# A fused attention and feed-forward kernel: V earlier in the prologue, transposes in separate PSUM tiles, V of one batch loaded in blocks, and a last tile in halves

## The chip, the cores and the metric

The kernel runs on one core of one Trainium2 chip. The metric is device microseconds of one execution. Each kernel is run several times on one chip beside the kernel before, and each run also leaves the span of the core and the mean clock that TensorE was granted. The span in a profile is 1.7 to 1.9 us shorter than the time of the same run. Positions "at 72 us" are counted from the start of the span.

## The reference

Eight batches of eight heads, 576 positions, head size 64: causal attention in a sliding window of 64. Its result, read as 4608 rows of 512, goes through a feed-forward stage (FFN) in which two products are multiplied by each other.

```python
scores = scale * np.matmul(q, k.transpose(0, 1, 3, 2))
mask = (rel >= 0) & (rel < 64)                      # rel = query - key position
attn = softmax(np.where(mask, scores, -1e9))
x = np.matmul(attn, v) -> (4608, 512)
a = x @ w1                                          # 512 x 1024
b = x @ w2
h = a * b @ w3                                      # 1024 x 1024
out = h @ w_out                                     # 1024 x 512
```

There is nothing non-linear behind `a * b`, so the kernel folds `w3 @ w_out` into one matrix of 1024 x 512 first, and each group of 512 rows then needs `a`, `b` and one product with the folded matrix.

## The kernel before

The order on each engine is the order in which the program writes it. Loads that cast to fp16 go through GpSimd's queue; K and Q of later batches come over SyncE's queue as fp32 and are cast on an engine. K, Q and V are transposed on TensorE into a PSUM tile and copied to SBUF by VectorE or ScalarE. V loaded as rows (`load_rows`) is transposed twice, to bring positions onto partitions; V loaded in blocks (`load_v`) comes from DRAM in its final place. The masks run on GpSimd.

```python
def load_v(b, *blocks):                              # V in blocks: no cast, no transpose
    vh = v_heads(b)
    for c in blocks:
        lo = D if c == 4 else 0
        s0 = VBLK[c] + lo
        nc.gpsimd.dma_start(out=vh[lo:P, c], in_=v[b, :, s0:s0 + P - lo, :].rearrange("h s d -> s h d"))

def transposes(b, which, *cs, into=None, cps=None):  # 6 transposes and one copy for each third c
    ...
    if into is None:
        into = [ps_t.tile([P, 6, P], FP16, name="tp")]      # ps_t has one buffer
    for c, tp in zip(cs, into):
        for i in range(6):
            nc.tensor.transpose(tp[:, i, :], t16[:, 6 * c + i, :], ident16)
    ...
    for c, tp, cp in zip(cs, into, cps):
        cp(dst..., tp...)

def scores(d):                                       # 16 matmuls, exp on ScalarE, masks on GpSimd
    ...
    nc.scalar.activation(pt[:, :, :, 0:w], s_ps[:, :, :, 0:w], AF.Exp, bias=-SHIFT, scale=scale)
    ...
        nc.gpsimd.affine_select(...)                 # two for each tile (four for a first tile)

def ffn_o(g, t):
    ab = abs_[g]
    o_ps = ps_f.tile([P, DM], FP32, name="f_ps")
    for fc in range(8):
        nc.tensor.matmul(o_ps, ab[:, fc, t * P:t * P + P], wc_sb[:, fc, :], start=(fc == 0), stop=(fc == 7))
    o_sb = sb.tile([P, DM], FP32, name="t2k", bufs=3)
    dve_cp(o_sb, o_ps)
    r0 = g * GT + t * P
    stores.append((r0, o_sb))

def spare(pool, name):                               # two places of one tile
    t = pool.tile([P, 2, 1024], FP16, name=name)
    return [t[:, i, 0:768].rearrange("p (i n) -> p i n", i=6) for i in range(2)]

def keep_busy(n):                                    # filler: computes nothing
    d = ps_t.tile([P, P], FP32, name="tp")
    for _ in range(n):
        nc.tensor.matmul(d, ident16, ident16, start=True, stop=True)
```

The prologue (batch 0 and the folding of the weights), cut:

```python
keep_busy(75)
tps = spare(ps_s, "s_ps") + spare(ps_v, "o_ps")
...                                                  # K of batch 0: cast, transpose, copy
keep_busy(10)
...                                                  # Q of batch 0 likewise
keep_busy(15)
scores(0)
keep_busy(12)
scores(1)
keep_busy(12)
fold_t(0)                                            # transposes of a piece of w3
scores(2)
fold_t(1, act_cp)
fold_mm(0, 0, dve_cp)                                # 8 matmuls of the folding
scores(3) ... scores(5)                              # with fold_t(2), fold_t(3), fold_mm(1..3, 0)
load_rows(1, "v")
keep_busy(12)
cast_qk(0, "v", 0, dve_cp)
cast_qk(0, "v", 1, dve_cp)
transposes(0, "v", 0, 1, 2, into=spare(ps_v, "o_ps") + [tp_bank()], cps=[dve_cp, act_cp, dve_cp])
...                                                  # rest of the folding, values(0..5)
transposes(1, "k", 0, 1, 2, into=spare(ps_s, "s_ps") + [tp_bank()])
ffn_ab(0, 0)                                         # first FFN matmuls
```

The stage after it, in which the first FFN group runs beside the attention of batch 1 and the preparation of batch 2:

```python
steps = [ffn_ab(0, 6), ffn_ab(0, 7)] + [ffn_o(0, t) for t in range(4)]     # shortened
for d in range(6, 12):
    values(d, ps_s if d in (9, 11) else None)
    if d < 9:
        scores(d + 3)
    steps.pop(0)()
    store()
    if d == 6:
        load_v(2, 4, 5)
        load_qk(3, "k")
    if d < 10:
        cast_qk(2, "kq"[(d - 6) // 2], d % 2, pool_cp)      # K of batch 2 is cast on GpSimd
    if d == 9:
        transposes(2, "k", 0)
    if d == 10:
        transposes(2, "k", 1)
transposes(2, "k", 2)
...
transposes(2, "q", 0, 1, 2, into=spare(ps_v, "o_ps") + spare(ps_s, "s_ps")[0:1])
```

Of the kernel before, what the change touches and what calls it, by code (L numbers as in the profile page):

```python
# [8 lines left out]
FP32 = mybir.dt.float32  # L9
FP16 = mybir.dt.float16  # L10
# [134 lines left out]
def kernel(  # L145
# [106 lines left out]
    def transposes(b, which, *cs, into=None, cps=None):  # L252

        t16 = t16s[which, b]
        if cs[0] == 0:
            turned[which, b] = sb.tile([P, NJ, S], FP16, name=which + "T", bufs=1 if which == "v" else 2)
        dst = turned[which, b]
        if into is None:
            into = [ps_t.tile([P, 6, P], FP16, name="tp")]
# [3 lines that stand above are left out]
        if cps is None:  # L263
            cps = [dve_cp if which == "k" or c != 1 else act_cp for c in cs]
        for c, tp, cp in zip(cs, into, cps):
            cp(dst.rearrange("q j (p i) -> q j p i", i=TI)[:, :, :, 6 * c:6 * c + 6],  # L266
               tp.rearrange("q i (p j) -> q j p i", p=TP))
# [172 lines left out]

    def ffn_o(g, t):
        ab = abs_[g]
        o_ps = ps_f.tile([P, DM], FP32, name="f_ps")
        for fc in range(8):
            nc.tensor.matmul(o_ps, ab[:, fc, t * P:t * P + P], wc_sb[:, fc, :], start=(fc == 0), stop=(fc == 7))  # L445
        o_sb = sb.tile([P, DM], FP32, name="t2k", bufs=3)
        dve_cp(o_sb, o_ps)  # L447
        r0 = g * GT + t * P
        stores.append((r0, o_sb))

    def store():
        while stores:
            r0, o_sb = stores.pop()
            nc.sync.dma_start(out=out[r0:r0 + P, :], in_=o_sb)

    wo16 = sb.tile([P, 8, DM], FP16, name="ab", bufs=3)
    w3a = sb.tile([P, 8, DM], FP16, name="ab", bufs=3)
# [11 lines left out]
    def load_wo(half):  # L469
        cols = slice(half * 256, half * 256 + 256)  # L470
        nc.gpsimd.dma_start(out=wo16[:, :, cols], in_=moe_w_out[:, cols].rearrange("(e p) m -> p e m", p=P))

    def load_w3(n):
        fc = 2 * n
        dst = w3a[:, 2 * fc:2 * fc + 4, :].rearrange("p (f a) n -> p f (a n)", f=2) if n < 2 else \
            xT[:, fc - 4:fc - 2, 2 * S:2 * S + DF]
        nc.gpsimd.dma_start(out=dst, in_=moe_w3[fc * P:fc * P + 2 * P].rearrange("(f p) n -> p f n", p=P))
# [40 lines left out]
    def keep_busy(n):  # L518
# [4 lines that stand above are left out]
# [7 lines left out]
    def ones_of(i):  # L530
        nc.gpsimd.memset(v16s[i].rearrange("p c j (a e) -> p (c j a) e", a=2)[:, :, D:2 * D], 1.0)

    ones_of(0)
    ones_of(1)
    load_wo(0)
    load_w3(0)
    load_w3(1)
    load_rows(0, "v")
    load_w3(2)
    load_w3(3)  # L540
    load_wo(1)

    def spare(pool, name):

        t = pool.tile([P, 2, 1024], FP16, name=name)
        return [t[:, i, 0:768].rearrange("p (i n) -> p i n", i=6) for i in range(2)]

    def tp_bank():
        return ps_t.tile([P, 6, P], FP16, name="tp")

    keep_busy(75)
    tps = spare(ps_s, "s_ps") + spare(ps_v, "o_ps")
    for c in range(3):
        cast_third(0, "k", c, act_cp if c == 1 else dve_cp)
    transposes(0, "k", 0, 1, 2, into=tps, cps=[dve_cp, act_cp, dve_cp])
    keep_busy(10)
    for c in range(3):
        cast_third(0, "q", c, act_cp if c == 1 else dve_cp)
    transposes(0, "q", 0, 1, 2, into=[tps[3], tp_bank(), spare(ps_s, "s_ps")[0]], cps=[act_cp, dve_cp, act_cp])
    keep_busy(15)  # L560
    scores(0)
    keep_busy(12)
    scores(1)
    for i in range(2):
        load_w12(i, 0)
    keep_busy(12)
    fold_t(0)
    scores(2)
    fold_t(1, act_cp)
    fold_mm(0, 0, dve_cp)  # L570
    scores(3)
    load_rows(1, "k")
    fold_t(2)
    fold_mm(1, 0, act_cp)
    scores(4)
    fold_t(3)
    fold_mm(2, 0, act_cp)
    scores(5)
    load_rows(1, "q")
    for i in range(2):  # L580
        load_w12(i, 1)
    load_rows(1, "v")
    fold_mm(3, 0, act_cp)
    keep_busy(12)
    cast_qk(0, "v", 0, dve_cp)
    cast_qk(0, "v", 1, dve_cp)
    transposes(0, "v", 0, 1, 2, into=spare(ps_v, "o_ps") + [tp_bank()], cps=[dve_cp, act_cp, dve_cp])
    fold_t(4, act_cp)
    fold_t(5)
    keys_of_v(0, [0, 1], spare(ps_v, "o_ps"), [act_cp, dve_cp])  # L590
    fold_mm(4, 0, act_cp)
    keys_of_v(0, [2, 3], spare(ps_s, "s_ps"), [act_cp, dve_cp])
    fold_t(6)
    fold_mm(5, 0, dve_cp)
    fold_t(7, act_cp)
    values(0)
    fold_mm(6, 0, dve_cp)
    values(1, ps_s)
    fold_mm(7, 0, dve_cp)
    for d in range(2, 6):  # L600
        values(d, ps_s if d % 2 else None)
        fold_mm(2 * d - 4, 1, dve_cp, 2)
        if d == 4:
            for hh in range(2):
                cast_qk(1, "k", hh, dve_cp)
    for n in range(3):
        keep_sums(n)


    transposes(1, "k", 0, 1, 2, into=spare(ps_s, "s_ps") + [tp_bank()])  # L610
    ffn_ab(0, 0)
    for hh in range(2):
        cast_qk(1, "q", hh, dve_cp)
    ffn_ab(0, 1)
    transposes(1, "q", 0, 1, 2, into=spare(ps_v, "o_ps") + [tp_bank()])
    ffn_ab(0, 2)
    scores(6)
    cast_qk(1, "v", 0, dve_cp)
    cast_qk(1, "v", 1, dve_cp)
    ffn_ab(0, 3)  # L620
    scores(7)
    load_qk(2, "k", nc.gpsimd.memset)
    load_qk(2, "q")
    transposes(1, "v", 0, 1, 2, into=spare(ps_v, "o_ps") + [tp_bank()], cps=[dve_cp, act_cp, dve_cp])
    ffn_ab(0, 4)
    scores(8)
    load_v(2, 0, 2, 3)
    keys_of_v(1, [0, 1, 2], spare(ps_v, "o_ps") + [tp_bank()], [dve_cp, act_cp, dve_cp])
    ffn_ab(0, 5)
    keys_of_v(1, [3], [tp_bank()], [act_cp])  # L630
    steps = [lambda fc=fc: ffn_ab(0, fc) for fc in range(6, 8)] + [lambda t=t: ffn_o(0, t) for t in range(4)]
    for d in range(6, 12):
        values(d, ps_s if d in (9, 11) else None)
# [6 lines that stand above are left out]
            load_qk(3, "k")  # L640
        if d < 10:
            cast_qk(2, "kq"[(d - 6) // 2], d % 2, pool_cp)
        if d == 9:
            transposes(2, "k", 0)
        if d == 10:
            transposes(2, "k", 1)
    transposes(2, "k", 2)
    for hh in range(2):
        cast_qk(3, "k", hh, pool_cp)
    transposes(2, "q", 0, 1, 2, into=spare(ps_v, "o_ps") + spare(ps_s, "s_ps")[0:1])  # L650
    load_qk(3, "q")
    copy_v(2, 1)
    copy_v(2, 4)
# [68 lines left out]
```

## Time and profile before

| Kernel before | |
|---|---|
| time, median of 4 runs | 293.74 us (292.65 to 294.05) |
| span of the profiled run, mean granted clock | 293.3 us, 0.989 |
| start of K's transposes of batch 1, then of the first FFN matmul | 45.52 and 46.52 us |
| first transpose of K of batch 2 | 73.50 us |
| first matmul of the second FFN group | 80.32 us |
| start of the last matmul | 287.40 us |

The last four lines cut the span into a prologue, a stage with the first FFN group, a long middle in which TensorE hardly ever waits, and an end. (The prediction counts from 45.37 us, where TensorE starts to load K as weights for its transposes; the first transpose itself is at 45.52.) A change is read by these marks: whatever it does must show as a shift between two of them. TensorE is busy for 96% of the span, so nothing is gained by making another engine faster for its own sake. But in the stage around 60 to 73 us TensorE follows GpSimd, and in the prologue it follows casts and copies. The prediction below shows these lines of the profile.

### The profile page before, as it was taken

How to read it: one execution, taken by the hardware profiler on the slowest of the kernel's cores; microseconds unless marked ns; L12 is line 12 of the kernel's file. 1: busy time of each engine (PE TensorE's matmuls, PEld its weight loads, DVE VectorE, ACT ScalarE, POOL GpSimd, SP SyncE). 2: the span in 40 equal slices, each digit the busy share in tenths (PEclk: the TensorE clock that was granted, in tenths of full speed). 3: DMA queues.
4: the chain of work that ended last, by engine and by line, in shares of the span. 5: the costliest groups of instructions: out<-in, count | busy, mean ns of one | idle time of the engine just before them, and what ended most of it. 6: DMA issues, size and time to landing. Idle time of an engine off the chain costs nothing.

```text
span 293.3 us, 6375 instructions
## 1 busy us (share of the span) xinstructions
PE 281.0 (96%) x2494; PEld 165.4 (56%) x2494; DVE 185.3 (63%) x284; ACT 168.4 (57%) x278; POOL 176.5 (60%) x212
## 2 busy tenths in 40 slices
PE   7698999999999999999999999999999999999992
PEld 7677886464644555555555787555555444444440
DVE  1627458845787567688777866577868555555531
ACT  2466742686258647766686565487568866641300
POOL 8779800589769857695879363786595344401200
PEclk9989999999999999999999999999999999999997
DMA  6999993079997939094839560950094012012012
GB/s 242 222 210 204 209 209 74 3 230 303 144 335 204 65 121 345 6 99 135 317 24 102 170 258 2 158 71 1 22 176 34 0 72 75 0 38 109 0 44 106
DMA packets 43906, 37.69 MB, mean 128 GB/s; under 512 B 29488, under 2 KB 33584, under 8 KB 43872
## 3 DMA queue, kind: packets, MB, share of 16 engines
q0 software_dynamic: 34560, 11.14, 36.0%
q1 hardware_dynamic: 9312, 26.10, 24.6%
q8 instruction: 20, 0.33, 0.4%
q14 instruction: 14, 0.11, 0.1%
HBM read 38.80 MB, written 9.44 MB: 164 GB/s over the span
## 4 chain that ended last, share of the span: by engine, by line
PE 84%; DVE 6%; POOL 4%; issue 2%; ACT 1%; POOLq 0%; ACTq 0%
PE f_ps L432 37%; PE f_ps L445 20%; PE o_ps L354 5%; PE tp L262 5%; PE s_ps L296 5%; PE f_ps L496 4%; PE tp L522 4%; POOL v L241 1%; DVE kT L266 1%; DVE k L226 1%; POOL pt L308 1%; PE o_ps L262 1%; PE f_ps L487 1%; DVE qT L266 1%; POOL k L226 1%
## 5 line engine op out<-in xcount | busy, mean ns | idle before, releaser
L432 PE MATMUL f_ps<-xT,w_sb 128*128 128x512 f16 (+1 forms) x640 | 134.2, 358 | 0.0
L308 POOL TENSOR_SCALAR_AFFINE_SELECT pt<-pt 128x512 f16<-128x512 f16 (+1 forms) x64 | 52.6, 822 | 77.2 <-ACT pt L300 77.2
L432 PEld LDWEIGHTS <-w_sb 128*128 128x128 f16 x640 | 59.7, 98 | 50.3 <-issue 0.3
L445 PE MATMUL f_ps<-wc_sb,ab 128*128 128x512 f16 x288 | 67.0, 379 | 0.1
L438 DVE TENSOR_TENSOR ab<-f_ps,a_sb 128x512 f16<-128x512 f32 x72 | 49.8, 691 | 19.2 <-PE f_ps L432 14.4
L437 ACT COPY a_sb<-f_ps 128x512 f32<-128x512 f32 x72 | 41.7, 579 | 27.0 <-PE f_ps L432 26.3
L300 ACT ACTIVATE pt<-s_ps 128x1024 f16<-128x1024 f32 (+1 forms) x48 | 45.6, 951 | 19.9 <-PE s_ps L296 18.2
L310 POOL TENSOR_SCALAR_AFFINE_SELECT pt<-pt 128x512 f16<-128x512 f16 (+1 forms) x64 | 52.1, 814 | 4.4
L363 DVE TENSOR_TENSOR xT<-o_ps,r 64x384 f16<-64x384 f32 x36 | 19.8, 550 | 39.7 <-ACT r L362 39.7
L445 PEld LDWEIGHTS <-ab 128*128 128x128 f16 x288 | 26.6, 98 | 28.4 <-issue 0.3
L360 ACT ACTIVATE ln_s<-o_ps 64x384 f32<-64x384 f32 x36 | 17.5, 487 | 32.6 <-PE o_ps L354 32.6
L447 DVE COPY t2k<-f_ps 128x512 f32<-128x512 f32 x36 | 24.8, 690 | 12.2 <-PE f_ps L445 11.7
L241 POOL DMA_DIRECT2D v<-in_v_dram x30 | 25.4, 854 | 0.0
L354 PEld LDWEIGHTS <-v 128*128 128x128 f16 x288 | 18.1, 98 | 8.7 <-ACT pt L300 0.8
L354 PE MATMUL o_ps<-pt,v 128*128 128x128 f16 (+1 forms) x288 | 20.7, 215 | 0.4 <-DVE xT L364 0.4
L364 DVE TENSOR_TENSOR xT<-o_ps,r 64x384 f16<-64x384 f32 x36 | 20.2, 561 | 0.5
L296 PEld LDWEIGHTS <-kT 64*128 64x128 f16 x384 | 10.6, 95 | 17.2 <-issue 15.6
L362 ACT ACTIVATE r<-ln_s 128x384 f32<-128x384 f32 x36 | 18.8, 522 | 1.1
L296 PE MATMUL s_ps<-qT,kT 64*128 64x128 f16 (+1 forms) x384 | 18.5, 217 | 0.3 <-DVE qT L266 0.3
L266 DVE COPY kT<-tp 128x768 f16<-128x768 f16 x19 | 18.1, 951 | 0.7 <-PE tp L262 0.7
L361 ACT ACTIVATE ln_s<-o_ps 64x384 f32<-64x384 f32 x36 | 17.4, 482 | 0.4
L226 POOL CAST k<-stage 128x1152 f16<-128x1152 f32 x12 | 13.8, 1151 | 1.7 <-PE tp L262 1.7
(87 smaller groups left out, 249.9 us busy)
## 6 DMA issues: line engine op xcount, KB each, us to landing
out_dram<-t2k SPq DMA_DIRECT2D x36, 256.0 KB
stage<-in_k_dram SPq DMA_DIRECT2D x14, 576.0 KB
stage<-in_q_dram SPq DMA_DIRECT2D x14, 576.0 KB
v<-in_v_dram POOLq DMA_DIRECT2D x24, 128.0 KB, 4.3
w_sb<-in_moe_w_dram POOLq DMA_DIRECT2D x4, 512.0 KB, 11.0
rows<-in_v_dram POOLq DMA_DIRECT2D x4, 288.0 KB, 11.5
ab<-in_moe_w_out_dram POOLq DMA_DIRECT2D x2, 512.0 KB, 12.0
ab<-in_moe_w_dram POOLq DMA_DIRECT2D x2, 512.0 KB, 8.9
```

What stands on the lines that cost most here:

```text
L241: nc.gpsimd.dma_start(out=vh[lo:P, c], in_=v[b, :, s0:s0 + P - lo, :].rearrange("h s d -> s h d"))
L266: cp(dst.rearrange("q j (p i) -> q j p i", i=TI)[:, :, :, 6 * c:6 * c + 6], tp.rearrange("q i (p j) -> q j p i", p=TP))
L296: nc.tensor.matmul(s_ps[:, a, jj, c0:c0 + n], kT[half, j, k0:k0 + P], qT[half, j, q0:q0 + n], start=True, stop=True, skip_group_check=True)
L300: nc.scalar.activation(pt[:, :, :, 0:w], s_ps[:, :, :, 0:w], AF.Exp, bias=-SHIFT, scale=scale)
L308: nc.gpsimd.affine_select(out=sl, in_=sl, pattern=pat, compare_op=ALU.is_ge, fill=0.0, base=off, channel_multiplier=-1)
L310: nc.gpsimd.affine_select(out=sl, in_=sl, pattern=[[-s, m] for s, m in pat], compare_op=ALU.is_ge, fill=0.0, base=63 - off, channel_multip ...
L354: nc.tensor.matmul(o_ps[:, jj, o0:o0 + n], v16[:, si * 2 + bi, j0 + jj, a * D:a * D + P], pt[:, a, jj, c0:c0 + n], start=first, stop=(bi = ...
L432: nc.tensor.matmul(d[:, f * n + c0:f * n + c1], w[:, dc, (fc + f) * P:(fc + f + 1) * P], xT[:, dc, xc:xc + c1 - c0], start=first, stop=(dc ...
L437: act_cp(a_sb[:, 0:nf * n], a_ps[:, 0:nf * n])
L438: nc.vector.tensor_tensor(ab[:, fc:fc + nf, lo:hi], b_ps[:, 0:nf * n].rearrange("p (f n) -> p f n", f=nf), a_sb[:, 0:nf * n].rearrange("p ...
L445: nc.tensor.matmul(o_ps, ab[:, fc, t * P:t * P + P], wc_sb[:, fc, :], start=(fc == 0), stop=(fc == 7))
L447: dve_cp(o_sb, o_ps)
```

## The change

The intent: get V of batch 0 sooner by loading it ahead of most of w3, let VectorE and ScalarE copy transposed parts without waiting for each other by giving each part a PSUM tile of its own, drop filler, save the cast and 42 transposes for V of batch 1 by loading it in blocks, and shorten the end by computing and storing the last tile in two halves. The core of the diff:

```diff
 def ffn_o(g, t):
+    halves = [(0, DM, dve_cp)] if (g, t) != (NG - 1, 3) else [(0, 256, act_cp), (256, DM, dve_cp)]
+    for c0, c1, cp in halves:
+        o_ps = ps_f.tile([P, DM], FP32, name="f_ps")
+        ...                                     # 8 matmuls for columns c0 to c1, then cp, then
+        stores.append((r0, c0, c1, o_sb))       # the first half's store goes to ScalarE's queue
...
+    load_w3(0)
     load_wo(0)
-    load_w3(0)
-    load_w3(1)
     load_rows(0, "v")
-    load_w3(2)
-    load_w3(3)
+    for n in range(1, 4):
+        load_w3(n)
...
+    def three():                                # one tile for each third
+        return [bank(ps_v, "o_ps"), tp_bank(), bank(ps_s, "s_ps")]
...
-    keep_busy(15)
+    keep_busy(6)
     scores(0)
-    keep_busy(12)
+    keep_busy(6)
+    fold_t(0)
     scores(1)
+    fold_t(1)
...
     scores(4)
-    fold_t(3)
-    fold_mm(2, 0, act_cp)
+    cast_qk(0, "v", 0, dve_cp)
+    cast_qk(0, "v", 1, act_cp)
+    keep_busy(6)
+    transposes(0, "v", 0, 1, 2, into=[bank(ps_v, "o_ps"), tp_bank(), bank(ps_f, "f_ps")], cps=[dve_cp, act_cp, dve_cp])
     scores(5)
...
-    load_rows(1, "v")
+    load_v(1, 0, 2, 3)
...
-    transposes(1, "k", 0, 1, 2, into=spare(ps_s, "s_ps") + [tp_bank()])
     ffn_ab(0, 0)
+    transposes(1, "k", 0, 1, 2, into=three(), cps=[dve_cp, act_cp, dve_cp])
...
+    ffn_ab(0, 3)
     scores(6)
-    cast_qk(1, "v", 0, dve_cp)
-    cast_qk(1, "v", 1, dve_cp)
-    ffn_ab(0, 3)
+    copy_v(1, 1)
...
-    transposes(2, "q", 0, 1, 2, into=spare(ps_v, "o_ps") + spare(ps_s, "s_ps")[0:1])
+    transposes(2, "q", 0, 1, 2, into=three())
```

## The prediction

> **What bounds the kernel now.** I read the page first, then the order of time engine by engine, the chain of work that ended last, and the busy time by windows.
>
> ```profile
> PE 281.0 (96%) x2494; PEld 165.4 (56%) x2494; DVE 185.3 (63%) x284; ACT 168.4 (57%) x278; POOL 176.5 (60%) x212
> ```
>
> TensorE is busy for 281.0 of 293.3 us, so a part pays only where it removes TensorE work or one of its few waits. From 100 to 280 us TensorE is never idle for more than 0.05 us and the change touches nothing there. What can move lies in three places: 0 to 46 us (weights folded, batch 0), 46 to 80 us (first FFN group beside batch 1), and the last 6 us. Here is the first, TensorE alone in order of time (start, duration, what, count, wait before it):
>
> ```profile
> 13.34 1.49 PE L522 MATMUL tp<-ident 128*128 128x128 f16 x15 [0.71 <-DVE qT L266]
> 14.77 0.50 PE L296 MATMUL s_ps<-qT,kT 64*128 64x128 f16 x8
> 15.20 1.46 PE L522 MATMUL tp<-ident 128*128 128x128 f16 x12
> 16.59 0.50 PE L296 MATMUL s_ps<-qT,kT 64*128 64x128 f16 x8
> 17.03 0.85 PE L522 MATMUL tp<-ident 128*128 128x128 f16 x12
> ...
> 24.82 0.83 PE L522 MATMUL tp<-ident 128*128 128x128 f16 x12
> 25.93 0.84 PE L262 MATMUL o_ps<-ident,k 128*128 128x128 f16 x12 [0.28 <-DVE k L226]
> ...
> 28.79 0.83 PE L273 MATMUL o_ps<-ident,vT 128*128 128x128 f16 x12 [0.78 <-DVE vT L266]
> ```
>
> L522 is filler that computes nothing; "k" at 25.93 is V of batch 0 (it shares that buffer). Some filler delays real work: the scores at 14.77 could have run at 13.7. V waits for its casts on VectorE (23.45 to 25.88 us), not for its load: its two DMAs landed at 19.6 and 21.0.
>
> In the second place GpSimd sets the pace. The chain of work that ended last, start and length:
>
> ```profile
> 61.44 0.49 POOL pt L310
> 61.93 0.48 issue
> 62.48 2.67 POOL v L241 x3
> 65.16 1.12 POOL pt L308
> ...
> 67.39 1.59 POOL v L241 x2
> 68.97 1.16 POOL k L226
> 70.13 1.06 POOL pt L308
> 71.25 1.10 POOL pt L310
> 72.35 1.10 POOL k L226
> 73.50 0.51 PE tp L262 x6
> ```
>
> From 60.27 (first mask of the ninth score tile) to 73.44 GpSimd works without a pause: masks, five loads of V of batch 2 to issue, two casts of K of batch 2. At 73.50 TensorE, which had waited 0.85 us, transposes that K. TensorE work removed ahead of 73.5 us comes back as a longer wait there unless this GpSimd row starts sooner too.
>
> The clock, one window of a microsecond each (the last three numbers are granted clock, DMA share, GB/s):
>
> ```profile
> 12.00:13.00 1.00, 0.63 (x12) 0.51 (x10) 0.72 (x2) 1.00 (x2) 0.55 (x1) 1.00 1.14 196
> 14.00:15.00 1.00, 1.00 (x14) 0.80 (x14) 0.00 (x0) 0.00 (x0) 0.00 (x0) 0.50 1.09 203
> ```
>
> Clock is halved from about 13.7 to 17.1 us; that is what the filler is for.
>
> **What the Trainium skill says.** "TensorE: Matmul & The Clock Gate", Part 1, says the clock falls to half after an idle window of some 3.4 us and recovers after a busy one. The trace agrees: half clock lasts 3.4 us, after a stretch with TensorE idle from 9.96 to 11.45 and partly to 13.3. Part 4 says transposes do not count as busy in the same way; the 18 transposes in that stretch did not prevent the fall, which fits but proves nothing. "GPSIMD Engine Reference", section 1, says GpSimd shares its SBUF interfaces with VectorE; the same 128x1152 fp16 copy took 450 to 1345 ns on VectorE, the longest under GpSimd masks. "DMA: Bandwidth & Descriptors", section "Specifications", says transfers below 512 B are inefficient. V in blocks moves 128 B per head and row; I check below that there is room.
>
> **The change, part by part.**
>
> *Order of loads.* Loads on GpSimd's queue land one after another, 2.5 us for a w3 or w_out piece and 1.4 for half of V. w3(0) moves from 15.7 to about 13.2, V from 21.0 to about 18.5. Folding starts at 15 us, so both suffice. Nothing on the path is gained by itself; it permits the new order.
>
> *Filler.* 136 becomes 109: 27 fewer, 9+6+6+6 of them, at 107 ns under half clock and 56 ns else. Worth about 2.5 us if nothing else waited.
>
> *Separate PSUM tiles.* ScalarE's K copy waited for VectorE's (2.7 us of idle, start 10.10) since both parts lay in one tile. Now it starts at 9.3. But VectorE still does two K copies of 0.95 in a row and ends near 10.9, and the third Q copy ends at 13.4 as before (ScalarE: two casts of 0.83, two copies of 0.81, from 10.1). No gain in the result.
>
> *The new prologue, worked with measured durations.* Q ready 13.4, six fillers, scores(0) at 13.85 (was 14.77). Filler and transposes of w3 at half clock, scores(1) at 15.85, scores(2) at 17.3 (was 18.26). From here a score tile needs 0.40 matmul, 1.02 exp and 0.15 of handover, at least 1.57: scores(3) at 18.95, scores(4) at 20.5 (were 20.09, 21.85). So 1.3 us ahead. But now half of the V cast stands on ScalarE behind exp(4), 20.97 to 21.99, and takes 1.1 to 1.15 (scaled from 0.81 for 768 and 1.01 for 1024 elements): V's transposes start at 23.25, after 2.0 us of TensorE idle. Before they started at 25.93, but by then scores(5), two w3 transposes and two folds were done as well, 0.45+2x0.45+2x0.93 = 3.2 us. Left after 23.25: 18.5 us (what stood from 25.93 to 45.37, less its 0.94 wait) + 3.2 = 21.7 us. New waits: 0.65 for the V copies (two of 0.95 on VectorE); 0.65 and 0.55 where a fold waits for a w3 copy that VectorE does only after a multiply of values (Ln 0.50, exp 0.52, multiply 0.56, copy 0.69 against 2.4 us of TensorE work). Start of FFN: 23.25 + 21.7 + 1.85 = 46.8 us, against 45.37. **+1.4 us.**
>
> *V of batch 1 in blocks.* It removes 42 transposes (42 x 56 ns = 2.4 us of TensorE), two casts, three copies of V to its transposed form and four back. It adds three 64-row copies of 0.29 on VectorE, and on GpSimd five issues of 0.7 to 0.9 us in place of two of 0.59, at 33 to 39 us, where GpSimd was idle from 36 to 54.6. Loads stood through at 47.9 us; five blocks at 0.85 to 1.3 us end by 51, and the first use is near 56. No harm. But the gain meets the GpSimd row. From the start of FFN: the seventh score tile now comes after four FFN steps instead of three, 9.2 us (was 7.9); its masks start at 10.5 (was 9.3), and those of the ninth at 15.3 (was 14.9). The row then takes 13.17 us as before: K of batch 2 is transposed 28.5 us after the start of FFN, before 28.1. TensorE arrives there at 25.75 and waits 2.7 us instead of 1. **+0.4 us, the 2.4 us saved spent in waiting.**
>
> *Last tile in halves.* The last VectorE copy shrinks from 0.69 to 0.41 (128x256 as in the fold), and the last store is half of 256 KB, whose packets took 0.85 us. **-0.6 us.**
>
> Sum: +1.4 + 0.4 - 0.6 = +1.2, so 295.0 us.
>
> **The rivals.** (1) TensorE work decides: 2.5 us of filler, 2.4 of transposes and 0.6 at the end vanish, giving 288.5 to 290.5. For it: TensorE is 96% busy. Against: the two waits above, on ScalarE behind exp(4) and on GpSimd at 60 to 73 us, which less TensorE work cannot shorten. A half way, in which my waits for V are half as long and VectorE keeps up, gives 293. (2) The clock: with TensorE idle 2.0 us at 21.3 and 2.7 us near 72 us it may fall again, or, with less filler, recover at 20.5 rather than 17.1. Each costs about 1.7 us (3.4 us at half speed): 296.5 to 298. For it: the fall at 13.7. Against: at 27.4 to 30.9 a stretch of mostly transposes and a wait of 0.9 cost no clock. (3) The small packets of V delay the second halves of w1 and w2: these stand ahead in the same queue, so no change.
>
> **Range and chances.** My working gives 295.0; a kernel changed in so many places by someone with a chip at hand is more likely to be no worse, so I take 294.6. Rival 1 in part sets the low end, rival 2 once the high end: 292.0 to 296.9. 2% is 5.9 us, which needs rival 1 in full or rival 2 three times.
>
> **What would show it.** Right: V of batch 0 transposed at about 23.3 after 2 us of TensorE idle; first FFN matmul near 46.8; K of batch 2 transposed after a TensorE wait of 2 to 3.5 us put down to GpSimd's cast; 27 fewer fillers and 42 fewer transposes; the end 0.6 us shorter after the last matmul. Wrong: FFN starting before 45, a wait at K of batch 2 under 1 us, or half clock after 20 us.

## The result, and the profile after

| | before | after |
|---|---|---|
| time, median of 4 runs | 293.74 us (292.65 to 294.05) | 297.71 us (297.36 to 298.36) |
| ratio, 95% interval | | 1.0145 (1.0112 to 1.0177) |
| span and clock of the profiled run | 293.3 us, 0.989 | 295.6 us, 0.985 |

The ratio is the mean time of one kernel's runs over the mean of the other's in the same rounds, so it is not quite the ratio of the medians. The changed kernel is slower by 1.4%: above the range I gave (292.0 to 296.9) and 3.1 us above the predicted time.

First the page of the changed kernel: the busy times, and TensorE's granted clock in 40 slices of 7.4 us (tenths of full speed).

```profile
PE 278.6 (94%) x2433; PEld 163.1 (55%) x2433; DVE 180.6 (61%) x281; ACT 168.1 (57%) x276; POOL 178.9 (61%) x215
...
PEclk9999999998699999999999999999999999999998
```

TensorE has 61 matmuls and transposes fewer and is busy for 2.4 us less, yet the span is 2.3 us longer. So waits have grown by more than the work has shrunk, and part of what work is left ran slower: in the tenth and eleventh slice (66 to 81 us) the clock falls to 0.8 and 0.6. The kernel before has nothing of the kind there.

The prologue, TensorE alone in order of time (start, duration, engine, line, operation, out<-in, count, wait before it and who ended it):

```profile
13.20 0.49 PE L527 MATMUL tp<-ident 128*128 128x128 f16 x6 [0.72 <-DVE qT L266]
...
21.83 0.51 PE L262 MATMUL o_ps<-ident,k 128*128 128x128 f16 x6 [1.71 <-ACT k L226]
...
24.35 0.50 PE L273 MATMUL o_ps<-ident,vT 128*128 128x128 f16 x6 [0.45 <-DVE vT L266]
...
44.90 1.89 PE L432 MATMUL f_ps<-xT,w_sb 128*128 128x512 f16 x8
```

V's transposes wait 1.71 us for the half of the cast that stands on ScalarE behind an exp, as predicted. L527 is the filler: at 13.20 six of them took 0.49 us, which is full clock. This execution had no fall of the clock in the prologue at all, where the profiled run of before had 3.4 us of it. That is chance, as the experiments show, and it makes 44.90 look better than the new prologue is.

The stage with the first FFN group. The chain of work that ended last, start and length:

```profile
66.83 1.57 POOL v L241 x2
68.39 1.15 POOL k L226
69.54 1.06 POOL pt L308
...
70.67 1.09 POOL pt L310
71.76 1.10 POOL k L226
...
72.91 0.82 PE tp L262 x6
```

It is the same GpSimd row as before, less than a microsecond sooner: load issues, cast of K, two masks, cast of K, and then the transposes of K of batch 2. TensorE around it:

```profile
67.80 1.90 PE L450 MATMUL f_ps<-wc_sb,ab 128*128 128x512 f16 x8
72.91 0.82 PE L262 MATMUL tp<-ident,k 128*128 128x128 f16 x6 [3.21 <-POOL k L226]
...
74.65 3.59 PE L450 MATMUL f_ps<-wc_sb,ab 128*128 128x512 f16 x8
...
82.91 0.49 PE L262 MATMUL tp<-ident,q 128*128 128x128 f16 x6 [0.97 <-DVE kT L266]
```

Three things are to be seen. The wait for K is 3.21 us, where in the kernel before it was 0.85 (at 73.50 us, line below). After it, the same eight matmuls take 3.59 us instead of 1.90, and six transposes 0.82 instead of 0.51. And there is a second wait, 0.97 us at 82.91, that the kernel before has not: the middle third of Q goes to the tile `tp`, which has one buffer and still holds the last third of K, not copied yet. In the kernel before:

```profile
73.50 0.51 PE L262 MATMUL tp<-ident,k 128*128 128x128 f16 x6 [0.85 <-POOL k L226]
```

The granted clock of the changed kernel (third number from the right; then DMA share and GB/s) in windows of 2 us settles the slow matmuls:

```profile
72.00:74.00 2.00, 1.09 (x14) 0.90 (x16) 0.24 (x1) 0.00 (x0) 1.93 (x3) 0.50 1.89 226
74.00:76.00 2.00, 2.00 (x18) 1.00 (x15) 0.88 (x2) 1.01 (x2) 2.00 (x2) 0.50 1.80 196
...
78.00:80.00 2.00, 2.00 (x26) 1.36 (x25) 1.58 (x2) 0.49 (x1) 0.00 (x0) 0.82 0.07 28
```

Half clock lasts from 71.9 to 78.7 us, 6.83 us in all (the last window holds its end). By the marks, the two profiled runs differ like this. To compare starts of the stage, I count the 18 transposes of K of batch 1 into it in both kernels; before they stand ahead of the first FFN matmul (1.00 us), after behind it.

| stretch | before | after | difference |
|---|---|---|---|
| start to the stage | 45.52 | 44.90 | -0.62 |
| stage to second FFN group | 34.80 | 38.68 | +3.88 |
| second group to last matmul | 207.08 | 206.82 | -0.26 |
| last matmul to end of span | 5.93 | 5.23 | -0.70 |

The sum is +2.3 us, which is the difference of the spans. It is less than the 4.0 us between the medians because the profiled run of before was a slow one of its kind (295.06 us, 1.3 over its median) and that of after a fast one (297.36, 0.35 under). So the two profiles alone do not show the whole loss, and single marks have to be compared over more runs.

### The profile page after: what moved, and what is told of

Read it like the earlier page. It is cut to its first block, busy times and chain, and to the rows that moved or that the text cites. A ratio compares the mean times of both kernels' runs of the same rounds, so it can differ in the third digit from the quotient of the medians.

```text
span 295.6 us, 6258 instructions
## 1 busy us (share of the span) xinstructions
PE 278.6 (94%) x2433; PEld 163.1 (55%) x2433; DVE 180.6 (61%) x281; ACT 168.1 (57%) x276; POOL 178.9 (61%) x215
## 4 chain that ended last, share of the span: by engine, by line
PE 87%; ACT 4%; DVE 4%; POOL 2%; issue 1%; POOLq 0%; DVEq 0%; ACTq 0%
PE f_ps L432 41%; PE f_ps L450 21%; PE tp L262 5%; PE o_ps L354 5%; PE s_ps L296 5%; PE f_ps L501 4%; PE tp L527 3%; PE o_ps L338 1%; ACT pt L300 1%; POOL k L226 1%; PE f_ps L492 1%; DVE xT L346 1%; DVE vT L266 1%; ACT r L345 1%; ACT q L229 1%
## 5 line engine op out<-in xcount | busy, mean ns | idle before, releaser
L450 PE MATMUL f_ps<-wc_sb,ab 128*128 128x512 f16 (+1 forms) x296 | 68.7, 380 | 0.1
L450 PEld LDWEIGHTS <-ab 128*128 128x128 f16 x296 | 27.8, 99 | 28.9 <-issue 2.2
L452 DVE COPY t2k<-f_ps 128x512 f32<-128x512 f32 (+1 forms) x36 | 24.5, 682 | 13.9 <-PE f_ps L450 13.5
L241 POOL DMA_DIRECT2D v<-in_v_dram x35 | 29.6, 853 | 1.8 <-DMA rows<-in_k_dram 1.1
L266 DVE COPY kT<-tp 128x768 f16<-128x768 f16 x18 | 17.1, 951 | 3.4 <-PE tp L262 3.3
```

The source lines that it names most:

```text
L450: nc.tensor.matmul(o_ps[:, 0:c1 - c0], ab[:, fc, t * P:t * P + P], wc_sb[:, fc, c0:c1], start=(fc == 0), stop=(fc == 7))
L452: cp(o_sb[:, c0:c1], o_ps[:, 0:c1 - c0])
```

## The experiments

My theory before them had four parts: (a) the wait for GpSimd's casts at K of batch 2 costs time by itself, and (b) through the clock, which falls in it; (c) the shared tile at Q costs almost a microsecond; (d) the new prologue is longer than the old one, and the profiled run hid that. The rivals: the clock falls there for some other reason than the wait; the five small-packet loads of V slow something; the prologue is level and all the loss lies in the stage. All twelve kernels gave right results. "Before" is the median of the kernel before in the same rounds.

| kernel | median us (range) | before | ratio (95%) |
|---|---|---|---|
| x1_q_bank | 296.74 (293.68 to 297.61) | 293.51 | 1.006 (0.9987 to 1.0134) |
| x2_filler | 296.48 (295.95 to 297.03) | 293.51 | 1.0081 (1.0028 to 1.0134) |
| x3_k_casts | 293.41 (292.17 to 294.76) | 293.51 | 0.9968 (0.9909 to 1.0026) |
| x4_blocks_only | 293.14 (292.70 to 293.67) | 293.51 | 0.9978 (0.9926 to 1.003) |
| y1_before_best | 290.45 (289.47 to 292.11) | 294.27 | 0.9867 (0.9833 to 0.9901) |
| y2_after_mended | 293.75 (292.54 to 294.45) | 294.27 | 0.9969 (0.9939 to 1.0) |
| y3_prologue_only | 297.06 (296.05 to 298.13) | 294.27 | 1.0089 (1.0057 to 1.0121) |
| y4_end_only | 294.00 (292.86 to 294.58) | 294.27 | 0.998 (0.9951 to 1.0009) |
| z1_after_clock | 296.18 (295.06 to 296.82) | 294.08 | 1.007 (1.0051 to 1.009) |
| z2_best_clock | 289.07 (288.54 to 290.98) | 294.08 | 0.9853 (0.9825 to 0.9882) |
| z3_casts_only | 292.77 (291.94 to 294.63) | 294.08 | 0.9974 (0.995 to 0.9997) |
| z4_best_whole_end | 290.55 (289.66 to 291.46) | 294.08 | 0.9871 (0.9854 to 0.9888) |

And the marks of each profiled run. "Stage" counts K of batch 1 into the stage, as above, so the start of the stage is the first transpose of that K (1.00 us ahead of the first FFN matmul) where the old order stands, and the first FFN matmul elsewhere.

| run | half clock before 90 us: start (length) | start of stage | stage |
|---|---|---|---|
| before | 13.67 (3.41) | 45.52 | 34.80 |
| after | 71.9 (6.83) | 44.90 | 38.68 |
| x1_q_bank | 13.01, 23.25, 74.45 (3.41 each) | 46.88 | 36.16 |
| x2_filler | 11.44 (6.83) | 46.74 | 35.97 |
| x3_k_casts | 12.68, 22.92 (3.41 each) | 46.89 | 33.76 |
| x4_blocks_only | 12.99 (3.41) | 44.97 | 33.63 |
| y1_before_best | 12.97 (3.41) | 44.94 | 31.42 |
| y2_after_mended | 12.49 (6.83) | 47.09 | 32.63 |
| y3_prologue_only | 12.68 (6.83) | 48.51 | 34.64 |
| y4_end_only | 12.70 (3.41) | 44.61 | 34.80 |
| z1_after_clock | 73.8 (3.41) | 44.58 | 37.65 |
| z2_best_clock | none | 43.54 | 31.40 |
| z3_casts_only | none | 43.38 | 33.77 |
| z4_best_whole_end | 13.41 (3.41) | 45.84 | 31.39 |

Within a run, half clock starts on a grid: in x1_q_bank the distances between starts are 10.24 and 51.20 us, which are 3 and 15 times 3.413 us. Where the grid lies differs from run to run. Each run also begins at half clock, up to 4.6 to 7.0 us (filler matmuls start 107 ns apart until then and 56 ns apart after); the table leaves that out.

Read after all the runs, the grid tells more. I cut each of the fourteen traces into its cells of 3.413 us and added up TensorE's busy time, transposes and filler included, in each. In the cell before every one of the 29 falls (those at the end of the program included) TensorE was busy for 1.57 us or less. In every one of the 1121 other cells that began at full clock it was busy for 1.60 us or more. Half clock ended after cells with 2.98 us or more and went on after cells with 2.94 us or less. Two cells of after (start:end, length, busy time and count of TensorE, granted clock, DMA share, GB/s):

```profile
68.48:71.90 3.42, 1.22 (x6) 1.00 1.33 321
20.70:24.11 3.41, 2.06 (x34) 1.00 1.12 211
```

The first holds most of the 3.21 us wait for K, and the clock fell at its end. The second holds the 1.71 us wait for V of batch 0, and the clock did not fall. In x1_q_bank the same wait of 1.71 us lies in a cell with 1.56 us of work, and there the clock fell. So what counts in these traces is whether one cell is left more than half empty, by some 1.8 us or more, and where a wait lies on the grid is chance. No run was set up to test this, and the ends of matmuls in a profile are modelled; the two sides of the line, 1.57 and 1.60 us, lie close.

### x1_q_bank: the shared tile at Q of batch 2

```diff
-    transposes(2, "q", 0, 1, 2, into=three())
+    transposes(2, "q", 0, 1, 2, into=[bank(ps_v, "o_ps"), bank(ps_f, "f_ps"), bank(ps_s, "s_ps")])
```

> The changed kernel, with the three banks for the transposes of Q of batch 2 chosen so that none is the one-buffer tile tp (two of the old ones and one of f_ps). Theory (the wait of 0.97 us at 82.9 us is for tp, which still holds the last third of K of batch 2): the wait goes, and the kernel is 0.5 to 1.1 us faster than the changed one, 296.6 to 297.2 us. Rival (the copies of K and Q on VectorE, three of 0.95 us in a row, set the next scores whatever bank is used): the wait only moves to the scores behind it, under 0.3 us gained, 297.5 us.

The wait of 0.97 us at Q is gone, and 0.31 us comes up at the next scores, which the kernel before has as well. From K of batch 2 to the second FFN group it took 83.04 - 74.89 = 8.15 us, of which some 1.3 are the half clock (0.31 at the transposes, 0.42 at the values, 0.59 at the eight matmuls, each from its start to the next start, against the same at full clock). The rest, 6.83, is the 6.82 us of before. So (c) is right, and this tile is the whole of what the change added behind K's transposes: in x2_filler, which has the tile and the full clock, the same stretch takes 82.71 - 74.75 = 7.96 us. Of these 1.14 us, 0.39 comes back because the 0.31 at the scores is not there (the stretch behind is 206.82 us in after and 207.21 here), which leaves about 0.75.

The timing by itself settles nothing, its interval holds 1. But the four runs show how far one kernel moves with its clock: they were 293.68 us at a mean clock of 0.997, and 296.57, 296.91 and 297.61 at 0.986, 0.983 and 0.978.

### x2_filler: hold the clock through the wait

```diff
         if d > 8:
+            if d == 9:
+                keep_busy(50)
             transposes(2, "k", d - 9)
```

> The changed kernel, with 50 filler matmuls (2.8 us at full clock) just ahead of the first third of the transposes of K of batch 2, where TensorE waited 3.2 us. Theory (the wait costs twice: 3.2 us of idle time, and then the half clock from 71.9 to 78.7 us that it brings): the wait is filled and not shortened, the clock stays at 1.00, and the kernel is 2.3 to 3.0 us faster than the changed one, about 295 us. Rival (only the GpSimd row decides, the half clock falls where TensorE has time): no difference, 297.7 us. If TensorE is on the path there, filler would cost up to 2.8 us.

TensorE around K of batch 2:

```profile
71.38 2.96 PE L527 MATMUL tp<-ident 128*128 128x128 f16 x50
74.75 0.51 PE L262 MATMUL tp<-ident,k 128*128 128x128 f16 x6 [0.42 <-POOL k L226]
...
75.76 1.90 PE L450 MATMUL f_ps<-wc_sb,ab 128*128 128x512 f16 x8
```

The filler lies inside the wait, K comes exactly as late after the first FFN matmul as in after (74.75 - 46.74 = 28.01 us; 72.91 - 44.90 = 28.01), and the work behind it runs at full clock. The stage is 35.97 us instead of 38.68. So the fall costs 2.7 us, and it does not come where TensorE is not empty: (b) holds: the two cells of the grid around K have 3.41 and 2.99 us of work here, where the one in after had 1.22. Part (a) falls: before, K came 73.50 - 45.52 = 27.98 us into the stage, so the wait only eats what the blocks save and costs nothing on top. The time fell by only 1.2 us against after (297.71 to 296.48, in different rounds; by the ratios, each to before in its own rounds, 1.9 us), less than the 2.3 to 3.0 us expected. The profiled run had two windows of half clock in the prologue, which that of after had not; whether the other runs had them, their mean clocks (0.984 to 0.990) don't tell.

### x3_k_casts: take K of batch 2 off GpSimd

```diff
         if d < 10:
-            cast_qk(2, "kq"[(d - 6) // 2], d % 2, pool_cp)
+            if d in (8, 9):
+                cast_qk(2, "q", d % 2, pool_cp)
+            if d == 8:
+                cast_qk(2, "k", 0, dve_cp)
+                cast_qk(2, "k", 1, act_cp)
```

> The changed kernel, with the two casts of K of batch 2 (1.15 us each) taken from GpSimd and given to VectorE and ScalarE. Theory (the GpSimd row holds TensorE up, and the half clock follows from that wait): the wait of 3.2 us at 72.9 falls under 0.8 us, no half clock near 72 us, and the kernel is 4.5 to 6 us faster than the changed one, 291.7 to 293.2 us. Rival (K of batch 2 comes too late from memory, or the masks of the following score tiles are the next wait): at most 2 us gained, 295.7 us or more.

The wait at K is gone, and a shorter one for the masks takes its place, just behind (TensorE):

```profile
71.53 0.50 PE L262 MATMUL tp<-ident,k 128*128 128x128 f16 x6
73.13 0.64 PE L338 MATMUL o_ps<-pt,v 128*64 128x128 f16 x16 [1.11 <-POOL pt L310]
```

The clock holds, and the stage falls to 33.76 us: 4.9 less than after, 2.2 less than with the clock held by filler. This one edit of the changed kernel brings it back level with the kernel before: 293.41 us, ratio 0.9968 with an interval that holds 1 (4.3 us less than after, in different rounds, where I had expected 4.5 to 6). So a loss of that size could be taken back by moving two casts to other engines. That does not make these casts the whole cause: the edit also removes a wait that the kernel before has, and the longer prologue and the tile at Q are still there.

### x4_blocks_only: the kernel before with V of batch 1 in blocks

```diff
-    load_rows(1, "v")
+    load_v(1, 0, 2, 3, 4, 5)
...                       # and without the casts and both turns of V of batch 1
```

> The kernel before, with this one part of the change: V of batch 1 in five blocks straight to its place, the 42 transposes, casts and copies gone, the rest as before. Theory (TensorE gains 2.4 us, arrives earlier at the transposes of K of batch 2 and waits there for GpSimd): a wait of 2 to 3.5 us there instead of 0.85; if the clock holds 0.5 to 1.2 us faster than before (292.6 to 293.2 us), if it falls 1 to 2.5 us slower (294.7 to 296.2 us). Rival (the work removed is simply gained): 2.4 to 3 us faster, 290.8 to 291.3 us.

```profile
71.77 0.51 PE L262 MATMUL tp<-ident,k 128*128 128x128 f16 x6 [2.18 <-POOL k L226]
```

The wait at K of batch 2 grows from 0.85 to 2.18 us: more than half of the work saved on TensorE is spent waiting there. Some 1.2 us stay (stage 33.63 against 34.80). The clock did not fall at this wait in the profiled run; the wait was split between two cells of the grid, with 1.98 and 2.66 us of work. The timed gain, 0.4 us in the medians, is not separable from none. The loads in blocks do no harm: in the changed kernel the five land between 46.2 and 49.4 us, VectorE first copies from them at 54.8 and TensorE first reads them at 58.5.

### y1_before_best and z4_best_whole_end: blocks, with the casts off GpSimd

To the kernel before: V in blocks as in x4_blocks_only, K's casts as in x3_k_casts, and for y1_before_best the last tile in halves as in the change.

```diff
-    load_rows(1, "v")
+    load_v(1, 0, 2, 3, 4, 5)
...
+                cast_qk(2, "k", 0, dve_cp)
+                cast_qk(2, "k", 1, act_cp)
...                       # y1 only: ffn_o and store of the change
```

> The kernel before with V of batch 1 in blocks, the two casts of K of batch 2 moved from GpSimd to VectorE and ScalarE, and the last tile in halves; its own prologue kept. Theory (the blocks gain 2.4 us of TensorE work only if GpSimd no longer holds K of batch 2 up; the masks of the following score tiles then leave a wait of about 1 us): no wait over 1.5 us between 60 and 80 us, no half clock there, 2.5 to 4 us faster than before, 289.5 to 291 us. Rival (some other row, VectorE or the loads of batch 2, binds at the same place): under 1.5 us faster.

> The kernel y1 with its last tile in one piece again. Theory now, after y4 (the earlier copy is used up by the issues of two queues that overlap and by the wait for the write to land): within 0.3 us of y1, and from the end of the last matmul's stream to the end of the span 5.1 to 5.7 us in both. The prediction's view (0.6 us gained by halves): this one 0.5 to 0.7 us slower than y1.

TensorE in y1_before_best, where the other kernels wait:

```profile
69.41 0.50 PE L262 MATMUL tp<-ident,k 128*128 128x128 f16 x6
69.98 0.64 PE L338 MATMUL o_ps<-pt,v 128*64 128x128 f16 x16
```

No wait is left at K and hardly any behind it. The stage takes 31.42 us, 3.4 less than before, and the kernel is 1.3% faster than before. The halves add nothing to it: without them the same kernel takes 290.55 us (ratio 0.9871), with them 290.45 (0.9867).

### z3_casts_only: the casts off GpSimd, nothing else

```diff
+                cast_qk(2, "k", 0, dve_cp)
+                cast_qk(2, "k", 1, act_cp)
```

> The kernel before with only the two casts of K of batch 2 moved off GpSimd. Theory (the row of GpSimd holds TensorE up by 0.85 us there, no more): 0.5 to 1.0 us faster, 293.2 to 293.8 us, so that blocks and casts together gain over twice what the two gain apart. Rival (the casts are worth the 2 to 3 us by themselves): 291.5 us or less.

The stage is 33.77 us, 1.0 less than before; the time is 0.3% less, 0.9974 with an interval just below 1 (the medians lie 1.3 us apart). Blocks alone are worth 1.2 us in the stage, casts alone 1.0, both 3.4. They are two halves of one thing: less work on TensorE pays only if the GpSimd row that TensorE meets at K gets shorter as well, and a shorter row pays only as far as TensorE had waited for it (0.85 us before).

### y2_after_mended: the changed kernel with both repairs of the stage

To after: the tile of x1_q_bank, the casts of x3_k_casts, and filler in the wait for V of batch 0.

```diff
     cast_qk(0, "v", 1, act_cp)
-    keep_busy(6)
+    keep_busy(36)
     transposes(0, "v", 0, 1, 2, ...)
```

> The changed kernel with three repairs: casts of K of batch 2 off GpSimd, no tp tile in the transposes of Q of batch 2, and 36 instead of 6 fillers ahead of the transposes of V of batch 0, where TensorE idled for 1.9 us. Theory (the loss of the change is these two waits and the half clock they bring, and the new prologue is no faster than the old): 291.5 to 292.7 us, and no half clock near 23 us. Rival (the new prologue is worth 2 us once its clock is held): 289.5 to 290.5 us, the same as or better than the kernel before with the good parts.

The stage is repaired: 32.63 us. Yet the kernel takes 293.75 us and y1_before_best, which has the old prologue, 290.45 in the same rounds. There was no second fall, but the first at 12.49 us lasted two windows, and the stage began at 47.09 us, 2.15 later than in y1_before_best. What is lost now lies in the prologue, and that is more than I had expected (291.5 to 292.7 us).

### y3_prologue_only: the old kernel with the new prologue

```diff
-    load_wo(0)
     load_w3(0)
-    load_w3(1)
+    load_wo(0)
     load_rows(0, "v")
...                       # the whole new order up to the first FFN matmul, V of batch 1 still by rows
```

> The kernel before with the new prologue alone (order of loads, separate PSUM tiles, early V, 27 fillers fewer), V of batch 1 by rows and all that follows as before. Theory of the prediction (V's cast stands behind an exp on ScalarE, folds wait for copies on VectorE, and the clock falls once or twice): first FFN matmul up to 1.5 us later than before, allowing for the K transposes that stand behind instead of ahead of it; time 0 to 1.5 us slower, 293.5 to 295 us. Rival (27 fewer fillers are a gain): 1.5 to 2.5 us faster, 291 to 292 us.

It is 2.8 us slower than before (medians 297.06 and 294.27), more than I had expected. Part of that is my own splice: in the old order K of batch 1 is transposed ahead of the first FFN matmul, and the new prologue casts that K only after its last folds, so that TensorE waits 1.25 us, until 48.51 us, for a cast that the change itself never has to wait for there. Without it some 1.5 us are left, which is the predicted +1.4, but I only subtract here and do not show it.

### y4_end_only: the last tile in halves, nothing else

```diff
+    halves = [(0, DM, dve_cp)] if (g, t) != (NG - 1, 3) else [(0, 256, act_cp), (256, DM, dve_cp)]
...                       # ffn_o and store of the change
```

> The kernel before with the last tile in halves alone. Theory (the copy on the path shrinks from 0.69 to 0.41 us, the last store from 256 to 128 KB): from the start of the last matmul to the end of the span 5.2 to 5.4 us instead of 5.9, 0.5 to 0.7 us faster in the time. Rival (the end is set by the wait for the write to land and what follows, whatever its size): under 0.2 us.

294.00 us against 294.27; the ratio's interval holds 1. With y1_before_best against z4_best_whole_end that makes two pairs without a gain of the expected 0.6 us. The end of the profiled run of before, and then of after:

```profile
287.82 0.69 DVE L447 COPY t2k<-f_ps 128x512 f32<-128x512 f32 x1 [1.04 <-PE f_ps L445]
```

```profile
289.84 0.37 ACT L452 COPY t2k<-f_ps 128x256 f32<-128x256 f32 x1 [6.33 <-DMA out_dram<-t2k]
290.24 0.38 ACTq L459 DMA_DIRECT2D out_dram<-t2k  x1
290.71 0.42 DVE L452 COPY t2k<-f_ps 128x256 f32<-128x256 f32 x1 [1.05 <-PE f_ps L450]
```

The last copy is shorter by 0.27 us, as meant, and the data do land sooner. I read this over the runs that don't have the shared tile at Q: five with halves (x1_q_bank, y1_before_best, y2_after_mended, y4_end_only, z2_best_clock) and five without (before, x4_blocks_only, y3_prologue_only, z3_casts_only, z4_best_whole_end). From the second FFN group to the last landing it takes 209.98 to 210.84 us with halves, 210.47 on average, and 210.68 to 211.35, 211.01 on average, without: 0.54 us sooner. But from the last landing to the end of the span it takes 2.23 to 2.24 us in all nine kernels with halves, and 1.70 to 1.71 in all five without. So the whole stretch, from the second group to the end of the span, is the same: 212.22 to 213.07 us, 212.70 on average, with halves, and 212.39 to 213.06, 212.72 on average, without. The 0.70 us in the table above, from one pair of profiles, was chance.

The traces show where the 0.53 us go. At the end of the program SyncE waits for its eight DMA semaphores (counters that a landed transfer raises) one after another, in the same order in every run. The eight waits in before and then in y1_before_best (durations in ns, then the starts of the first and of the last in us):

```profile
L691 SPq EVENT_SEMAPHORE  x8: 17/17/17, 290.1 to 291.6; - x8
```

```profile
L697 SPq EVENT_SEMAPHORE  x8: 17/17/17, 286.9 to 287.4; - x8
```

The stores take the eight semaphores in turn. With a whole tile the last store has the eighth, and the other seven waits are over when it lands (291.63 us in before). The halves make one store more, so the last store has the first semaphore again, and the other seven waits stand behind its landing (286.90 us in y1_before_best), 0.53 us in all. It is so in all fourteen traces. SyncE's own issue of the last store took 0.49 to 0.73 us in eight of the nine kernels with halves, against 0.33 in z2_best_clock and in the five without; why stays open, and the landing is sooner all the same.

### z1_after_clock: filler for the prologue of the changed kernel

```diff
-    keep_busy(10)
+    keep_busy(30)                 # between K and Q of batch 0
...
-    keep_busy(6)
+    keep_busy(15, True)           # behind Q, in a tile of its own
...
-    keep_busy(6)
+    keep_busy(36)                 # in the wait for V of batch 0
```

> The changed kernel, with the waits of its prologue filled: 30 instead of 10 fillers between the transposes of K and Q, 15 fillers in an f_ps bank (which need not wait for tp) instead of 6 in tp after them, 36 instead of 6 ahead of V of batch 0. Nothing else. Theory (the new prologue itself is about level with the old one, and what it loses is one to two extra windows of half clock): no half clock before 60 us, first FFN matmul at 44.5 to 45.2 us (46.7 to 47.1 in four of the five traces of this prologue so far), time 1 to 2 us below the changed kernel, 295.5 to 296.7 us. Rival (the order of instructions and not the clock is what costs): first FFN matmul at 46.5 us or later, time as the changed kernel.

The prologue keeps its clock in this run, and the stage starts at 44.58 us. (In after it kept its clock without the filler, by chance, but this filler leaves no cell of the grid between 5 and 30 us with less than 2.81 us of work.) The time is 296.18 us, 1.5 less than after in its rounds (medians of different rounds), still 0.7% over before. In the stage the clock falls again behind a wait of 3.21 us, this time for one window (73.8 us, 3.41 long). That window costs 37.65 - 35.97 = 1.7 us against the held clock of x2_filler. I had expected the new prologue to be about level with the old one once neither loses its clock; the next kernel shows that it is not.

### z2_best_clock: the same filler in y1_before_best

```diff
-    keep_busy(10)
+    keep_busy(38)
...
-    keep_busy(15)
+    keep_busy(15, True)
```

> The kernel y1 (old prologue, blocks, casts of K of batch 2 off GpSimd, halves), with the same fillers between K and Q (38 instead of 10) and after Q (15 in an f_ps bank). Theory (the half clock from about 13 us costs the old prologue too): no half clock before 280 us, first FFN matmul about 1 to 1.5 us earlier than in y1, 288.8 to 289.8 us. Rival (fillers at half clock were only filling waits): no difference to y1, 290.4 us.

TensorE in the prologue:

```profile
8.80 2.01 PE L527 MATMUL tp<-ident 128*128 128x128 f16 x33
10.83 0.51 PE L262 MATMUL o_ps<-ident,q 128*128 128x128 f16 x6
```

The filler reaches up to Q's transposes without a gap, where the kernel before waits 1.49 us. No half clock is left in this run between the start and the last matmul, and 289.07 us is the fastest of all: 1.5% less than before. What the filler adds is less sure: z4_best_whole_end, which lacks it, had 290.55 us in the same rounds, but the intervals of the two ratios overlap (0.9825 to 0.9882, 0.9854 to 0.9888). And z3_casts_only, with the old prologue as it was, had no fall there either, since its emptiest cell of the grid had 1.60 us of work. The stage starts at 43.54 us; in z1_after_clock, with the new prologue and likewise no fall, at 44.58. The pair without extra filler and without a fall, z3_casts_only and after, has 43.38 and 44.90. So at equal clock the new prologue costs 1.0 to 1.5 us: (d) is shown, by profiles of single runs.

## Why the prediction was wrong

Point by point, with its own steps:

**The new prologue, "+1.4 us": right in kind, its exact size in part luck.** The V transposes followed a wait for ScalarE's half of the cast, 1.71 us where I had 2.0, and the first FFN matmul stood at 46.74 to 46.89 us in x1_q_bank, x2_filler and x3_k_casts where I had 46.8. But each of these has two windows at half clock, and my working had one. At full clock the stage starts at 44.58 to 44.90 us; with one window it would be some 45.8, half way, which is an estimate, since no run of this prologue had just one. The waits were shorter than I had them (0.45, 0.43 and 0.34 us in after for my 0.65, 0.65 and 0.55), and the second window made up for it. At full clock the cost is 1.0 to 1.5 us (44.58 against 43.54, 44.90 against 43.38). With the clocks of these runs it is 46.84 us on average in the three, against 45.18 in the five runs with the old prologue and one window: +1.7.

**V in blocks, "+0.4 us, the 2.4 us saved spent in waiting": right in kind, a bit too dark.** I had TensorE waiting 2.7 us for the cast of K of batch 2, and put 2 to 3.5 us as the mark; it was 3.21. K's transposes started 28.01 us into the stage where I had 28.5, and 27.98 before, so this is 0.0 and not +0.4.

**The clock, left out of the sum: this is the step that failed.** I named the fall near 72 us as the second rival, priced one at "about 1.7 us (3.4 us at half speed)", and then set it aside because "at 27.4 to 30.9 a stretch of mostly transposes and a wait of 0.9 cost no clock". That was the wrong comparison: a wait of 0.9 us (0.78 in the line that I showed) says nothing on one of 2.7 that I predicted myself. The runs show the fall at 71.9 us, over two windows rather than one, and x2_filler prices it at 2.7 us; for one window z1_after_clock gives 1.7, just the price that I had. The mechanism was in the prediction; what it lacked was a place in the sum. Half clock after 20 us was one of my own signs of being wrong, and it came.

**Separate PSUM tiles, "No gain in the result": incomplete.** I checked them in the prologue only. The same helper is used for Q of batch 2, where it puts a third of Q into a tile with one buffer that K has just filled. That is the 0.97 us wait, about 0.75 us net, and it can be read from the diff's last hunk: a tile name that two neighbours in the program use is a wait.

**Last tile in halves, "-0.6 us": right up to the landing, wrong for the end.** The last data land 0.54 us sooner, but the program ends no sooner: 212.70 and 212.72 us in five runs each. I had left out SyncE's waits at the end, of which seven now stand behind the last landing (0.53 us).

**The shading from 295.0 to 294.6** rested on who might have made the change and on no line of the profile; it went the wrong way.

With the measured terms the sum is: prologue +1.0 to +1.5 at equal clock, blocks 0, Q's tile +0.75, halves 0, the fall at 72 us +2.7. That is +4.5 to +5.0, against +4.0 measured (293.74 to 297.71). The rest is of the size by which the prologue's clock moves one kernel from run to run: before itself had medians from 293.51 to 294.27 in these rounds, with runs from 292.24 to 295.26.

What stays open: how often the clock falls at each place, since only one run of each kernel was profiled. In those with the change's wait of some 3 us at K of batch 2 and no filler there (after, x1_q_bank, z1_after_clock) it fell in all three, for one or two windows. An estimate from the cells above: if all else in a cell is work and a fall needs 1.84 us of it empty (3.41 less 1.57), a wait of 3.21 us costs the clock in some 85% of its positions on the grid, my 2.7 us in some 70%, the 2.18 us of x4_blocks_only in some 55%, and one of 1.71 us only where other idle time lies beside it.

The first rival, that TensorE's work decides, was not wrong about the worth of the saving: y1_before_best gets 3.4 us out of the stage with it. It needs the GpSimd row out of the way, which the change did not do.

## What to carry to other kernels

When a change takes work off the busiest engine, look for the next place where that engine meets another one: the saving turns into a wait there unless the other's row shortens too, so move both in one step. A wait of some microseconds on TensorE is paid twice if its clock falls in it; put the fall into the sum, as an expected cost, for every predicted wait that can leave a 3.41 us cell more than half empty, and fill what waits can't be removed. When the end of a program is to be shortened, read what the program still waits for after the last landing. And compare prologues only between runs whose granted clock is the same, since one profile may have been lucky.

## What the Trainium skill lacked or had wrong

- "TensorE: Matmul & The Clock Gate", Part 1, gives as its rule that TensorE should have no idle gap above about 3.4 us (its closing table says about 3). That is too lax for what these runs show: the clock fell at 71.9 us within a wait of 3.21 us, and at 23.25 and 22.92 us (x1_q_bank, x3_k_casts) behind a wait of 1.7 us. The same wait of 1.7 us cost no clock in after, x2_filler and y3_prologue_only, nor did 2.18 us in x4_blocks_only. That section does say that the window runs free, and the grid of 3.413 us seen within x1_q_bank agrees. What the page lacks is how full a window must be: in these fourteen traces the clock fell after 1.57 us of work or less, and not after 1.60 us or more.
- The same part has the clock back after one busy window. That agrees here if busy means nearly full, which the page does not say: half clock ended after windows with 2.98 us of work or more, and lasted a second window where the first had 2.40 to 2.94 us (after, x2_filler, y2_after_mended, y3_prologue_only).
- Part 4 says that transposes don't count as busy in the same way. In these traces they do count: the window of after from 20.70 to 24.11 us has 2.06 us of work, 1.73 of it transposes, and the clock did not fall, while it fell after one of x3_k_casts (19.50 to 22.92) with 1.57 us of work and no transpose in it.
- "DMA: Bandwidth & Descriptors", section "Issuing engines are not separate DMA queues", says that issuing from several engines saves only the issue time, which is usually small. The page lacks that an issue can also take longer: SyncE's last one took 0.49 to 0.73 us with ScalarE's just ahead of it in eight kernels and 0.33 in a ninth, against 0.33 without. Whether the two hinder each other no run shows.
- No page has what the end of this program showed: eight waits for DMA semaphores in a fixed order, some 0.07 us each, of which seven stood behind the last landing with 37 stores and none with 36 (2.23 against 1.70 us to the end of the span).
